# Start order, one transposed load and the last output segment of a one-core state-space and MLP kernel

## Chip, cores and metric

The kernel runs on 1 core of one Trainium2 chip. The metric is the device time of the program in microseconds; lower is better. Times below are medians of repeated runs, and readings of single instructions come from one profiled execution.

A core has five engines that run their own instruction streams and meet at semaphores: TensorE (PE in the profile; its weight loads are shown as PEld), VectorE (DVE), ScalarE (ACT), GpSimd (POOL) and SyncE (SP), which here only issues transfers. Transfers can also be issued from ScalarE's and GpSimd's streams.

## What is computed

```python
# scan: batch 4, 8 heads, 768 steps, head_dim D = 32, state N = 16
log_a = np.log(np.clip(a, 1e-06, 1.0))
for c in range(nc):                       # chunks of 32 steps
    cum = np.cumsum(la, axis=-1)
    L = np.exp(cum[:, :, :, None] - cum[:, :, None, :]) * causal
    M = np.einsum('bhin,bhjn->bhij', Cc, Bc) * L
    y_intra = np.einsum('bhij,bhjd->bhid', M, xc)
    y_inter = np.einsum('bhin,bhnd->bhid', Cc, state) * np.exp(cum)[..., None]
    y[:, :, sl] = y_intra + y_inter
    decay_from_j = np.exp(cum[:, :, -1:] - cum)
    Bx = np.einsum('bhjn,bhjd->bhjnd', Bc, xc) * decay_from_j[..., None, None]
    state = np.exp(la.sum(-1))[:, :, None, None] * state + Bx.sum(axis=2)
# bridge: (batch, heads, steps, D) -> 3072 tokens x 256
x = y.transpose(0, 2, 1, 3).reshape(3072, 256)
# MLP: w_in 256 x 2048, w_out 2048 x 256
h = x @ w_in
out = (h * (1 / (1 + np.exp(-h)))) @ w_out
```

`moe_w_in` and `moe_w_out` arrive as 64-bit floats; the kernel turns them into 32-bit floats itself.

## The kernel before

**Units and pairs.** The 3072 tokens are cut into 12 units of 256 (`UT`), three to a batch. A unit goes through the scan, then through the first product (`w_in` and silu, eight slots j of 256 hidden features each), then through the second (`w_out`). From the third pair of units on, the first product works on two units at once with seven products of half size in place of eight (`f_x1`); the second product of every pair does the same (`s2_pair`, segments named 1, w, 5, 7, 6, 4 and 3, each of eight matmul steps).

**The scan of a unit**, chunks of 64 steps (`Q`), by the names in the code:
- `f_Ab` (L308) spreads the decays over the partitions with two matmuls into a PSUM tile `hp`; `f_Ek` (L315, the scan of L303) turns them into the decay matrix E on VectorE. This pair of functions is used for units 0 and 1 only.
- B is needed twice. `bn` has tokens on the partitions (`load_n`, L99); `f_B` (L337) multiplies it by the last column of E on GpSimd. BH has states on the partitions: unit 0 loads `tbc` in blocks (`load_t`, L109) and transposes the 32x32 blocks on VectorE (`f_T`, L343, stream transposes at L346); unit 1 transposes `bn` itself on TensorE (`f_TP`, L350) and copies the result on ScalarE (L358). `f_T` and `f_TP` make CT from C in the same two ways, and `f_T2` (L361) makes the two masked copies `ce`.
- `f_D0` (L374) makes each chunk's state contribution, `f_G0` (L395) the products of C and B in the PSUM tile `gy`; `f_P01` (L274) makes the prefix products of units 0 and 1 on VectorE from the load `pa01`; `f_S` (L417) chains the states on VectorE (L428, L430); `f_SM` (L433) masks them; `f_M` (L412) multiplies E by `gy`; `f_Y` (L448) makes the output of the scan; `f_X` (L473) copies it to XM, in two halves for units 0 and 1.

**Weights** come in 16 pieces (0 to 7 of `w_in`, 8 to 15 of `w_out`). `load_w` fetches the raw words, `w_size` (L160) makes u and v on ScalarE, `w_bits` (L168) makes three VectorE instructions (L174, L176, L178) and the adds on GpSimd (L182; in two halves if `parts` is 2), and then issues the load of the piece seven further on. Slot j of the first product needs piece j.

**Order.** The program is laid out by hand (`manual_schedule`): what an engine does and in which order is the order of the calls. The start is L795 to L849: unit 0's scan, unit 1's scan woven with pieces 0 to 5, and the first four slots of unit 0 (`f_s1(0, 0)` to `f_s1(0, 3)`, L487). Then `steps` (L851) lists the other slots of units 0 and 1 as (unit, slot, what follows): "b5" is `w_bits(5)`, "s6" is `w_size(6)`. `busy(n, small)` (L222) issues matmuls on zeros, n of 512 columns and `small` of 64, which fill TensorE's gaps.

**PSUM.** `ps_h` has three buffers (tiles `hp`), `ps_s` one (`gy`), `ps_o` one (tiles `o_ps`: those of `busy`, of `f_TP` and of the second product). A tile of a pool waits until the readers of the tile that had its buffer before are done.

**The end.** L951 to L958 run `s2_pair(P, True)` for the last pair. Its segments give 128 output features on the partitions and 256 tokens in the free dimension. `end` (L572) copies each to `ps` (L578; the copy undoes the order in which `f_X` left the chunks), sums them on VectorE (`p_add`), and `f_out` (L550) transposes 32x32 blocks on VectorE and issues four transfers on SP. The last segment, "3", is the exception (L591 to L607): twice, for 128 tokens each, VectorE adds segment 6, TensorE transposes, ScalarE or VectorE copies, and SP or ScalarE issues a transfer.

Of the kernel before, what the change touches and what calls it, by code (L numbers as in the profile page):

```python
# [8 lines left out]
FP32 = mybir.dt.float32  # L9
# [3 lines left out]
ALU = mybir.AluOpType  # L13
# [8 lines left out]
def kernel(  # L22
# [56 lines left out]
    def at(u):  # L79
        return u // UPB, u % UPB * UT  # L80
# [28 lines left out]
    def load_t(u, i, q):  # L109

        b, t0 = at(u)
        if i == 0:
            tbc[u] = loads.tile([128, 2, 2, 8, N], FP32, name="tbc")
        for g in range(4):
            q.dma_start(out=tbc[u][32 * g:32 * g + 32, i],
                        in_=(B, C)[i][b, 2 * g:2 * g + 2, t0:t0 + UT].rearrange("e (t r) n -> t e r n", r=8))
# [42 lines left out]

    def w_size(n):  # L160
        if n in raw:
            u = wu[n] = wtp.tile([128, 2, WF], FP32, name="wu")
            v = wv[n] = wtp.tile([128, 2, WF], FP32, name="wv")
            nc.scalar.activation(u, raw[n][:, :, :, 1].bitcast(FP32), AF.Abs)

            nc.scalar.activation(v, raw[n][:, :, :, 0], AF.Copy, scale=2.0 ** -51, bias=2.0)

# [27 lines left out]
    pz01, one01, pfx01 = (flat[:, 8 * UT + QZ * i:8 * UT + QZ * (i + 1)] for i in range(3))  # L195
    load_t(0, 0, nc.scalar)
    load_t(0, 1, nc.sync)
# [117 lines left out]
    def f_Ek(u, k):  # L315
        scan_E(u, H * k, H, ab.pop((u, k)))
# [33 lines left out]
    def f_TP(u):  # L350

        tp = ps_o.tile([128, 512], FP32, name="o_ps")
        for i, t in enumerate((bn[u], tbc.pop(u))):
            for k in range(2):
                nc.tensor.transpose(out=tp[:, 256 * i + 128 * k:256 * i + 128 * k + 128],
                                    in_=t[:, k].rearrange("p h n -> p (h n)"), identity=ident)
        BH[u] = sc.tile([128, UT], FP32, name="bh")
        nc.scalar.activation(BH[u], tp[:, 0:256], AF.Copy)  # L358
        CT[u] = tp[:, 256:512]

# [112 lines left out]
    def f_X(u):  # L473
# [5 lines left out]
        for i in range(0, 4, n):  # L479
            nc.scalar.activation(XM[u][:, i:i + n], y[:, i:i + n, 0:128], AF.Copy)  # L480

    def new_g():

        return gpool.tile([128, NF, UT], FP32, name="gT").rearrange("p (k j) t -> p k j t", k=2)
# [76 lines left out]
    def s2_pair(P, final=False, joint=False):  # L561
# [10 lines left out]
        def end(m, o):  # L572

            p[m] = ppool.tile([128, UT], FP32, name="ps")
            on = o.rearrange("p (c k t) -> p c k t", c=2, k=2)
            pn = p[m].rearrange("p (k c t) -> p c k t", c=2, k=2)
            if not (final and m == "3"):
                nc.scalar.activation(pn, on, AF.Copy)  # L578
            if m == "w":
# [8 lines left out]
            elif m == "4":  # L588
                p_add(p["4"], p["4"], p["7"], adder)
                PEND.append(partial(f_out, P, 1, 0, p["4"]))  # L590
            elif m == "3" and final:  # L591

                for k in range(2):
                    nc.vector.tensor_tensor(out=pn[:, :, k], in0=on[:, :, k],
                                            in1=p["6"].rearrange("p (k c t) -> p c k t", c=2, k=2)[:, :, k],
                                            op=ALU.add)

                    tp = ps_h.tile([128, 512], FP32, name="hp")[:, 0:128]
                    nc.tensor.transpose(out=tp, in_=p["3"][:, 128 * k:128 * k + 128], identity=ident)
                    ot = opool.tile([128, UT], FP32, name="ot")[:, 0:128]  # L600
                    if k == 0:
                        nc.scalar.activation(ot, tp, AF.Copy)
                    else:
                        nc.vector.tensor_copy(out=ot, in_=tp)
                    b, t0 = at(2 * P + 1)
                    r = b * S + t0 + 128 * k
                    (nc.sync, nc.scalar)[k].dma_start(out=out[r:r + 128, 0:128], in_=ot)  # L607
            elif m == "3":
                p_add(p["3"], p["3"], p["6"], adder)
                PEND.append(partial(f_out, P, 0, 1, p["3"]))  # L610
# [12 lines left out]
        for n, (m, w, g) in enumerate(segs):  # L623
            if joint and n < 2:
                continue
            if final and n % 2 == 0:
# [148 lines left out]
    def scan_plan(G):  # L775
        plan = [([], [], []) for _ in range(8)]
        for i in range(2):
# [10 lines left out]
            plan[j + 2][2].append(partial(f_Y, u))  # L788
            plan[j + 3][1].append(partial(f_X, u))
            if u + 1 < NU:  # L790
# [3 lines left out]

    for i in range(2):  # L795
        f_T(0, i)
    for e in range(2):
        f_T2(0, e)
    f_Ab(0, 0)
    f_Ab(0, 1)  # L800
    busy(0, 20)
    f_G0(0)
    busy(4, 8)
    f_Ek(0, 0)
# [12 lines left out]
    w_size(1)  # L817
    busy(4, 17)
    f_Y(0)
    f_Ab(1, 1)  # L820
    f_X(0)
# [3 lines left out]
    f_s1(0, 0)  # L825
    f_Ek(1, 0)
    f_TP(1)
# [12 lines left out]
    for k in range(2):  # L840
        f_M(1, k)
    f_s1(0, 2)
    w_size(4)
    w_bits(3, 2)
    w_bits(4)
    f_Y(1)
    f_X(1)
    w_size(5)
    f_s1(0, 3)  # L849

    steps = ((1, 0, "b5 s6"), (1, 1, "b6 s7"), (1, 2, "b7 s8"), (1, 3, "b8"), (0, 4, ""),  # L851
             (1, 4, "T"), (0, 5, "E D s9"), (1, 5, "C b9 s10"), (0, 6, ""), (1, 6, "G b10 s11"),
# [137 lines left out]
```

## Time and profile before

| | us |
|---|---|
| median of 5 runs | 351.89 (351.63 to 352.75) |
| the profiled execution | 351.78 |
| its span | 350.1 |
| TensorE busy | 343.7 |
| VectorE busy | 205.5 |
| ScalarE busy | 162.4 |
| GpSimd busy | 112.4 |

The span is the time from the first to the last instruction that the profiler saw; the device time has a little around it. A line of the order of time gives start, duration, engine, line, operation, out <- in, shapes and count; several instructions of one kind that follow each other are one line whose duration runs from the first start to the last end. In brackets stands how long the engine was idle before and what ended that. The end of a matmul is modelled, so consecutive matmuls overlap in the records; their starts are what counts.

### The profile page before, as it was taken

The numbers are of one execution on the slowest core, as the hardware profiler recorded it, in microseconds if no ns is written. First come the engines' busy times: TensorE is split into PE (matmuls) and PEld (weight loads), VectorE is DVE, ScalarE is ACT, GpSimd is POOL, SyncE is SP. The second block draws the span as 40 slices with busy tenths as digits, with TensorE's granted clock in tenths as the row PEclk, the third lists the DMA queues.
The fourth block names the chain that finished last, engine by engine and source line by source line (L and its number), as shares of the span: only waits on it lengthen the run. The fifth ranks groups of instructions, "written<-read, shape, count | busy, mean of one in ns | idle before, by whom it ended". The sixth has DMA issues, their size and how long they took to land.

```text
span 350.1 us, 8359 instructions
## 1 busy us (share of the span) xinstructions
PE 343.7 (98%) x3308; PEld 287.5 (82%) x3308; DVE 205.5 (59%) x408; ACT 162.4 (46%) x396; POOL 112.4 (32%) x140
## 2 busy tenths in 40 slices
PE   8989999999999999999999999999999999999995
PEld 3568888888888888888888888888888888888884
DVE  6998899976795664544663563664552231234812
ACT  2578495323323545455645454644545454454100
POOL 4344346444185032244042244042234112051200
PEclk9999999999999999999999999999999999999999
DMA  5878897699866798956189955057404237522202
GB/s 107 213 221 217 228 324 125 120 208 224 145 123 116 127 169 148 189 111 98 21 160 162 179 102 103 16 106 138 93 2 75 52 55 147 94 39 41 43 1 46
DMA packets 117376, 42.79 MB, mean 122 GB/s; under 512 B 102488, under 2 KB 109144, under 8 KB 117336
## 3 DMA queue, kind: packets, MB, share of 16 engines
q1 hardware_dynamic: 110328, 25.67, 35.5%
q0 software_dynamic: 4464, 16.25, 25.0%
q10 hardware_dynamic: 2544, 0.33, 0.6%
q8 instruction: 26, 0.43, 0.5%
q14 instruction: 14, 0.11, 0.1%
HBM read 22.83 MB, written 3.15 MB: 74 GB/s over the span
## 4 chain that ended last, share of the span: by engine, by line
PE 92%; SPq 4%; DMA 2%; DVE 1%; issue 0%; ACT 0%; ACTq 0%; POOL 0%; DVEq 0%
PE o_ps L631 36%; PE hp L686 28%; PE hp L495 15%; PE hp L631 3%; PE gy L467 3%; PE o_ps L617 2%; PE gy L458 2%; PE gy L404 2%; SPq L107 2%; PE gy L389 1%; SPq L156 1%; DMA tbc<-in_C_dram 1%; DMA tbc<-in_B_dram 1%; DMA out_dram<-ot 0%; SPq L556 0%
## 5 line engine op out<-in xcount | busy, mean ns | idle before, releaser
L689 DVE TENSOR_TENSOR gT<-hp,p 128x256 f32<-128x256 f32 x64 | 26.9, 420 | 73.8 <-ACT p L700 37.8
L631 PE MATMUL o_ps<-gT,w_out_sb 128*128 128x256 f32 x240 | 60.4, 379 | 0.0
L692 ACT ACTIVATE gT<-gT 128x256 f32<-128x256 f32 x96 | 39.7, 414 | 43.9 <-DVE gT L689 43.8
L495 PE MATMUL hp<-XM,w_in_sb 128*128 128x256 f32 x256 | 59.3, 381 | 0.3 <-POOL w_in_sb L182 0.3
L495 PEld LDWEIGHTS hp<-XM,w_in_sb 128*128 128x128 f32 x256 | 47.8, 190 | 8.1 <-POOL w_in_sb L182 1.1
L686 PE MATMUL hp<-raw 128*128 128x256 f32 x192 | 52.7, 380 | 0.0
L548 POOL TENSOR_TENSOR ps<-ps 128x256 f32<-128x256 f32 x35 | 29.3, 838 | 71.2 <-ACT ps L578 69.9
L631 PEld LDWEIGHTS o_ps<-gT,w_out_sb 128*128 128x128 f32 x240 | 45.4, 190 | 6.3
L543 POOL DMA_DIRECT2D gT<-gT x31 | 27.3, 911 | 66.3 <-DVE TN L534 21.5
L686 PEld LDWEIGHTS hp<-raw 128*128 128x128 f32 x192 | 36.2, 190 | 5.4 <-POOL ps L548 0.6
L700 ACT ACTIVATE p<-hp 128x256 f32<-128x256 f32 x64 | 24.5, 383 | 27.4 <-PE hp L686 25.9
L689 DVE TENSOR_TENSOR gT<-hp,u 128x256 f32<-128x256 f32 x32 | 13.6, 425 | 38.9 <-PE hp L686 38.9
L686 PE MATMUL hp<-XM,w_in_sb 128*128 128x256 f32 x128 | 34.1, 389 | 0.0
L497 ACT ACTIVATE gT<-hp 128x512 f32<-128x512 f32 x32 | 18.9, 592 | 25.2 <-PE hp L495 25.2
L686 PEld LDWEIGHTS hp<-XM,w_in_sb 128*128 128x128 f32 x128 | 23.3, 190 | 4.3 <-issue 1.0
L303 DVE TENSOR_TENSOR_SCAN E<-ab,diag 128x256 f32<-128x256 f32 (+1 forms) x32 | 25.3, 832 | 0.4
L578 ACT ACTIVATE ps<-o_ps 128x256 f32<-128x256 f32 x38 | 14.4, 382 | 23.9 <-PE o_ps L631 19.8
L340 POOL TENSOR_TENSOR BT<-bn,E 128x256 f32<-128x256 f32 x12 | 9.4, 784 | 48.4 <-DVE E L303 39.3
L631 PE MATMUL o_ps<-gT,wu 128*128 128x256 f32 x88 | 22.4, 380 | 0.0
L631 PE MATMUL o_ps<-gT,wv 128*128 128x256 f32 x88 | 22.2, 380 | 0.0
L631 PE MATMUL o_ps<-gT,raw 128*128 128x256 f32 x80 | 20.5, 380 | 0.0
L686 PE MATMUL hp<-raw,w_in_sb 128*128 128x256 f32 x64 | 19.1, 380 | 0.0
(125 smaller groups left out, 521.1 us busy)
## 6 DMA issues: line engine op xcount, KB each, us to landing
gT<-gT POOLq DMA_DIRECT2D x31, 512.0 KB, 6.2
ab<-in_a_dram SPq DMA_DIRECT2D x40, 128.0 KB, 3.2
raw<-in_moe_w_in_dram SPq DMA_DIRECT2D x8, 512.0 KB, 5.8
raw<-in_moe_w_out_dram SPq DMA_DIRECT2D x8, 512.0 KB, 5.9
xt<-in_x_dram SPq DMA_DIRECT2D x24, 128.0 KB, 5.4
out_dram<-ot SPq DMA_DIRECT2D x92, 32.0 KB, 1.7
bn<-in_B_dram SPq DMA_DIRECT2D x22, 64.0 KB, 3.8
tbc<-in_C_dram SPq DMA_DIRECT2D x40, 32.0 KB, 5.5
```

The costliest lines, as they stand in the source:

```text
L303: nc.vector.tensor_tensor_scan(out=E[u].rearrange("p k h t -> p (k h t)")[:, Q * g0:Q * (g0 + n)], data0=t.rearrange("p g t -> p (g t)"), ...
L467: nc.tensor.matmul(out=y[32 * q:32 * q + 32, 2 * w + c, 64 * k:64 * k + 64], lhsT=xc[64 * c:64 * c + 64, k, h], rhs=m[64 * c:64 * c + 64, ...
L495: nc.tensor.matmul(out=hp[:, i], lhsT=w_in_sb[:, kc, f * 128:(f + 1) * 128], rhs=xm[:, kc], start=(kc == 0), stop=(kc == KC - 1))
L497: nc.scalar.activation(GTS[g][:, :, j], hp, AF.Silu)
L543: nc.gpsimd.dma_start(out=o[:, js], in_=a[:, js], accum_op=ALU.add)
L548: engine.tensor_tensor(out=o, in0=p, in1=q, op=op)
L578: nc.scalar.activation(pn, on, AF.Copy)
L631: nc.tensor.matmul(out=o, lhsT=w(j), rhs=g()[:, j], start=(j == 0), stop=(j == last))
L686: nc.tensor.matmul(out=o, lhsT=w, rhs=x_, start=start, stop=True, skip_group_check=True)
L689: nc.vector.tensor_tensor(out=o, in0=p, in1=q, op=ALU.add)
L692: nc.scalar.activation(o, i, AF.Silu)
L700: nc.scalar.activation(o, i, AF.Copy)
```

## The change

Four edits.

1. **B of unit 0.** The blocked load of B for unit 0 (four transfers on ScalarE's queue) and its VectorE transpose go. `f_TP(0)` makes BH on TensorE and ScalarE from `bn`, behind unit 0's two `f_Ab`; C of unit 0 stays as it was. The fillers of the start are cut anew.
2. **E of unit 1.** `f_Ek(1, 0)` moves from behind `f_s1(0, 0)` to just behind `f_Y(0)`, that is ahead of `w_bits(1, 2)` on VectorE.
3. **Slots.** `f_s1(1, 0)` runs ahead of `f_s1(0, 3)`. `w_size(4)` is split: u where it was, v behind `f_X(1)`, and `w_bits(4)` behind that.
4. **The last segment.** In segment "3" of the last pair the activations are the stationary operand and the weights the moving one, so that tokens come out on the partitions: per half of 128 tokens eight products of 128 columns. Segment 6, which has to be added, is transposed by TensorE in the midst of the first half and copied to `ps`. Each half is then one VectorE add and one transfer on SP. So that 128 consecutive tokens lie together, the last pair's XM is written in token order (`f_XN`, two copies in place of one), and the last pair's `end` copies without reordering.

```diff
     def load_t(u, i, q):
...
-        if i == 0:
+        if u not in tbc:
             tbc[u] = loads.tile([128, 2, 2, 8, N], FP32, name="tbc")
...
-    def w_size(n):
+    def w_size(n, what="uv"):
         if n in raw:
-            u = wu[n] = wtp.tile([128, 2, WF], FP32, name="wu")
-            v = wv[n] = wtp.tile([128, 2, WF], FP32, name="wv")
-            nc.scalar.activation(u, raw[n][:, :, :, 1].bitcast(FP32), AF.Abs)
-
-            nc.scalar.activation(v, raw[n][:, :, :, 0], AF.Copy, scale=2.0 ** -51, bias=2.0)
+            if "u" in what:
+                u = wu[n] = wtp.tile([128, 2, WF], FP32, name="wu")
+                nc.scalar.activation(u, raw[n][:, :, :, 1].bitcast(FP32), AF.Abs)
+            if "v" in what:
+                v = wv[n] = wtp.tile([128, 2, WF], FP32, name="wv")
+
+                nc.scalar.activation(v, raw[n][:, :, :, 0], AF.Copy, scale=2.0 ** -51, bias=2.0)
...
-    load_t(0, 0, nc.scalar)
     load_t(0, 1, nc.sync)
     load_n(0, 0, nc.scalar)
...
     def f_TP(u):
 
         tp = ps_o.tile([128, 512], FP32, name="o_ps")
-        for i, t in enumerate((bn[u], tbc.pop(u))):
+        for i, t in enumerate((bn[u],) if u == 0 else (bn[u], tbc.pop(u))):
...
         nc.scalar.activation(BH[u], tp[:, 0:256], AF.Copy)
-        CT[u] = tp[:, 256:512]
+        if u > 0:
+            CT[u] = tp[:, 256:512]
...
+    def f_XN(u):
+
+        XM[u] = xmp.tile([128, 4, 128], FP32, name="XM")
+        y = DP.pop(u)
+        for w in range(2):
+            nc.scalar.activation(XM[u][:, 2 * w:2 * w + 2].rearrange("p k (c t) -> p c k t", c=2),
+                                 y[:, 2 * w:2 * w + 2, 0:128].rearrange("p c (k t) -> p c k t", k=2), AF.Copy)
...
             p[m] = ppool.tile([128, UT], FP32, name="ps")
-            on = o.rearrange("p (c k t) -> p c k t", c=2, k=2)
-            pn = p[m].rearrange("p (k c t) -> p c k t", c=2, k=2)
-            if not (final and m == "3"):
-                nc.scalar.activation(pn, on, AF.Copy)
+            if final:
+                nc.scalar.activation(p[m], o, AF.Copy)
+            else:
+                nc.scalar.activation(p[m].rearrange("p (k c t) -> p c k t", c=2, k=2),
+                                     o.rearrange("p (c k t) -> p c k t", c=2, k=2), AF.Copy)
...
-            elif m == "3" and final:
-
-                for k in range(2):
-                    nc.vector.tensor_tensor(out=pn[:, :, k], in0=on[:, :, k],
-                                            in1=p["6"].rearrange("p (k c t) -> p c k t", c=2, k=2)[:, :, k],
-                                            op=ALU.add)
-
-                    tp = ps_h.tile([128, 512], FP32, name="hp")[:, 0:128]
-                    nc.tensor.transpose(out=tp, in_=p["3"][:, 128 * k:128 * k + 128], identity=ident)
-                    ot = opool.tile([128, UT], FP32, name="ot")[:, 0:128]
-                    if k == 0:
-                        nc.scalar.activation(ot, tp, AF.Copy)
-                    else:
-                        nc.vector.tensor_copy(out=ot, in_=tp)
-                    b, t0 = at(2 * P + 1)
-                    r = b * S + t0 + 128 * k
-                    (nc.sync, nc.scalar)[k].dma_start(out=out[r:r + 128, 0:128], in_=ot)
...
+            if final and m == "3":
+
+                for c in range(2):
+                    ts = slice(128 * c, 128 * c + 128)
+                    o = ps_h.tile([128, 512], FP32, name="hp")[:, ts]
+                    for j in range(NF // 2):
+                        nc.tensor.matmul(out=o, lhsT=g()[:, j, ts], rhs=w(j), start=(j == 0), stop=(j == last))
+                        if c == 0 and j == 3:
+
+                            q = ps_h.tile([128, 512], FP32, name="hp")
+                            for k in range(2):
+                                tk = slice(128 * k, 128 * k + 128)
+                                nc.tensor.transpose(out=q[:, tk], in_=p["6"][:, tk], identity=ident)
+                            p[m] = ppool.tile([128, UT], FP32, name="ps")
+                            nc.scalar.activation(p[m], q[:, 0:UT], AF.Copy)
+                        if j == last:
+                            nc.vector.tensor_tensor(out=p[m][:, ts], in0=o, in1=p[m][:, ts], op=ALU.add)
+                            b, t0 = at(2 * P + 1)
+                            r = b * S + t0 + 128 * c
+                            nc.sync.dma_start(out=out[r:r + 128, 0:128], in_=p[m][:, ts])
+                        if j % 2:
+                            yield
+                continue
...
-            plan[j + 3][1].append(partial(f_X, u))
+            plan[j + 3][1].append(partial(f_XN if G == NU // 2 - 1 else f_X, u))
...
-    for i in range(2):
-        f_T(0, i)
+    f_T(0, 1)
     for e in range(2):
         f_T2(0, e)
     f_Ab(0, 0)
     f_Ab(0, 1)
-    busy(0, 20)
+    f_TP(0)
+    busy(0, 18)
     f_G0(0)
-    busy(4, 8)
+    busy(2, 10)
     f_Ek(0, 0)
...
     w_size(1)
-    busy(4, 17)
+    busy(3, 18)
     f_Y(0)
+
+    f_Ek(1, 0)
     f_Ab(1, 1)
     f_X(0)
     w_size(2)
     w_bits(1, 2)
     load_unit(2)
     f_s1(0, 0)
-    f_Ek(1, 0)
     f_TP(1)
...
     f_s1(0, 2)
-    w_size(4)
+    w_size(4, "u")
     w_bits(3, 2)
-    w_bits(4)
     f_Y(1)
     f_X(1)
+    w_size(4, "v")
+    w_bits(4)
     w_size(5)
-    f_s1(0, 3)
-
-    steps = ((1, 0, "b5 s6"), (1, 1, "b6 s7"), (1, 2, "b7 s8"), (1, 3, "b8"), (0, 4, ""),
+
+    steps = ((1, 0, ""), (0, 3, "b5 s6"), (1, 1, "b6 s7"), (1, 2, "b7 s8"), (1, 3, "b8"), (0, 4, ""),
```

## The prediction

> **What bounds the kernel now.** I read the page's parts 1 and 4 first, then a table of stretches, then the order of time at both ends.
>
> ```profile
> PE 343.7 (98%) x3308; PEld 287.5 (82%) x3308; DVE 205.5 (59%) x408; ACT 162.4 (46%) x396; POOL 112.4 (32%) x140
> PE 92%; SPq 4%; DMA 2%; DVE 1%; issue 0%; ACT 0%; ACTq 0%; POOL 0%; DVEq 0%
> 10.00:15.00 5.00, 4.52 (x113) 2.60 (x113) 4.75 (x12) 3.60 (x8) 1.39 (x2) 1.00 0.98 288
> 15.00:20.00 5.00, 4.59 (x21) 3.28 (x20) 4.97 (x7) 3.00 (x7) 3.08 (x5) 1.00 0.78 121
> 20.00:25.00 5.00, 4.31 (x142) 3.20 (x142) 4.69 (x12) 3.78 (x8) 1.70 (x3) 1.00 0.73 252
> 30.00:321.00 291.00, 291.00 (x2767) 248.27 (x2766) 165.87 (x336) 142.61 (x355) 96.01 (x111) 1.00 0.65 124
> 343.00:350.10 7.10, 3.51 (x16) 2.51 (x14) 1.62 (x5) 0.28 (x1) 0.00 (x0) 1.00 0.26 52
> ```
>
> In the stretches the columns are PE, PEld, DVE, ACT and POOL busy, then granted clock and DMA. From 25.5 to 345.9 us TensorE never pauses, and the change takes no matmul out of that stretch. So time can only come from the two ends: from when the solid stretch begins (before 25 us, where VectorE is busy 14.41 of 15 us and sets the pace) and from what follows the last matmul.
>
> ```profile
> 4.82 0.64 DVE L346 STREAM_TRANSPOSE bh<-tbc 128x256 f32<-128x256 f32 x1
> 8.74 0.46 DVE L276 TENSOR_SCALAR gT<-gT 128x512 f32<-128x512 f32 x1 [0.55 <-DMA gT<-in_a_dram]
> 11.76 0.72 PE L227 MATMUL o_ps<-gT 128*64 128x64 bf16 x17
> 13.18 0.43 DVE L176 TENSOR_SCALAR wu<-wu 128x512 uint32<-128x512 uint32 x1
> 14.58 0.83 DVE L176 TENSOR_SCALAR wu<-wu 128x512 uint32<-128x512 uint32 x1
> 15.34 1.21 DVE L178 SCALAR_TENSOR_TENSOR wv<-raw,wv 128x512 uint32<-128x512 uint32 x1
> 16.47 2.32 DVE L303 TENSOR_TENSOR_SCAN E<-hp,diag 128x512 f32<-128x512 f32 x2
> 16.63 1.40 POOL L182 TENSOR_TENSOR w_in_sb<-wu,wv 128x256 uint32<-128x256 uint32 x2 [0.63 <-DVE wv L178]
> 24.71 0.81 PE L467 MATMUL gy<-E,xt 64*32 64x64 f32 x60 [0.40 <-issue]
> ```
>
> The L176 of piece 0 takes 0.43 us; that of piece 1, beside GpSimd's adds (14.29 to 16.00), 0.83. The scans run beside the same adds in 2.32 for two, against 2.27 alone. The last line is a pause in unit 1's f_Y that nothing in the profile explains: its records stand still from about 24.1 to 24.7.
>
> ```profile
> 342.31 3.62 PE L631 MATMUL hp<-gT,raw 128*128 128x256 f32 x16
> 345.96 0.49 DVE L594 TENSOR_TENSOR ps<-hp,ps 128x128 f32<-128x128 f32 x2 [2.08 <-PE hp L631]
> 346.98 0.36 SPq L607 DMA_DIRECT2D out_dram<-ot  x1
> 347.58 0.37 ACTq L607 DMA_DIRECT2D out_dram<-ot  x1
> ```
>
> After the last matmul come an add, a transpose, a copy and a transfer, twice; the second copy also waits for an output buffer, so the last transfer is issued 1.62 us after the add starts, and the span ends 2.5 us after that issue starts.
>
> **The last segment.** Removed behind the last matmul: the step from add to last issue, 345.96 to 347.58 = 1.62 us. Put in its place: one add of 128 columns (the two of L594 take 0.49 overlapped, one 0.29) and 0.03 to the issue on SP, 0.32. Saved: 1.30. Added on TensorE ahead of it: two transposes of p["6"] (the four of L355 fill 37.69 to 38.13, 0.11 each) 0.22; their copy (0.38 on ScalarE) is hidden by the 0.9 us of matmuls left in the first half. And sixteen long instructions become thirty-two of half the columns, each with a full weight load. Today one takes 3.45/16 = 0.216. If half costs half, 32 x 0.108 = 3.45, no loss. No row of before has such a pair, a 128-column f32 load for 128 moving columns. The nearest balanced one is the filler L227, 64 weights for 64 columns: (0.72 - 0.20)/16 = 0.033 each, where L225's 512 columns run at (1.04 - 0.38)/3/512 = 0.43 ns a column, 0.0275 for 64. So a balanced pair pays some 5 ns: 32 x 0.113 = 3.62, +0.17. The bad bound is the load's own recorded length, 0.190 (L631 PEld), unhidden: 32 x 0.19 = 6.08, +2.63. I take +0.17, since L227 has the same balance. The first half's transfer queues on SP behind f_out's four issues, which end at 345.94, before the second half's at about 346.7, so it delays nothing. Net 1.30 - 0.22 - 0.17 = **0.9 us gained** (1.08 to -1.55).
>
> The Trainium skill speaks against this part: "TensorE: Matmul & The Clock Gate", section "Back-to-back issue gap", says that in a stream of load and matmul pairs 128 columns take about 81 ns where the matmul alone would take 56. By that ratio the estimate for 32 pairs is 5.0 us, and the segment would lose about 0.5 instead; the L227 row, 0.033 against 0.0275, has a much smaller ratio.
>
> **B of unit 0 by TensorE.** Removed: four transfers on ScalarE's queue (1.84 us of issuing) and one VectorE transpose (0.61 until the next starts). The B load for bn moves to 0.81 there, and SP sheds waits on outstanding transfers (0.5 and 0.3 at L115, 0.4 at L199, in SP's table of waits), so the prefix's input lands about 1 us sooner and L276's 0.55 wait goes. E's first scan starts near 5.4 instead of 5.92, but the second needs the second f_Ab, whose matmuls end at 6.81 either way: 6.85 to 7.98 against 8.19. Then the prefix, with no wait, is done at 9.7 instead of 10.4. Now the other side. f_TP(0) runs at 6.75 to 6.97, its copy on ScalarE at about 7.17 to 7.55, and the fillers behind it on TensorE write the same single o_ps buffer, so they wait until 7.6. From there 18 small (0.58), f_G0 (0.62), 2 large (0.43), 10 small (0.32) and three changeovers of 0.1 put f_D0 at 9.85 against 9.45, and its first result near 10.2, where VectorE's L428 stood at 10.39. Gain **0.2**; bounds 0.67, if f_D0 isn't late (9.72 for 10.39), and -0.2, if L428 needs all of f_D0's 0.45 and a late copy adds 0.25.
>
> **E between the pieces.** No instruction is added; 1.2 us of scan move ahead of piece 1. Lost beside GpSimd today: 0.40 and 0.52 on piece 1 (L176, L178), 0.31 on piece 2's L176 (0.74): 1.23. In the new order the adds of piece 0 run in 1.40 (the 16.63 row) under a 1.2 us scan, so piece 1's L174 meets their last 0.4; piece 2's L174 and L176 meet the last of piece 1's adds and f_B, 0.35 and 0.3. Some 1.05 remain: gain **0.15** (0 to 0.9, if no overlap is left but piece 2's). Piece 1 reaches GpSimd 0.2 us later by itself; s1(0,1) waits for it, and the 0.2 and 0.15 cover that. With both, f_M(1) ends near 22.9 instead of 23.2.
>
> **Slot order.** Today s1(0,3) follows f_Y(1) without a gap at 25.49 and so hides XM(1)'s copy (0.38 for each half). Slot (1,0) needs that copy: 0.2 to the last matmul's end, 0.38 of copy, less the overlap with the changeover, about 0.45 of idle TensorE. Against this, piece 3's first half leaves GpSimd at 24.71 + 0.73 = 25.44 today, no sooner than s1(0,3) needs it, so 0.1 to 0.15 would be lost in the old order anyway. Net cost **0.3** (bounds 0.5, and -0.1 if the 24.1 pause is gone and piece 3 would be the late one). Splitting piece 4's sizes takes 0.66 of ScalarE from in front of XM(1), which today waits for TensorE, not for them: nothing. Piece 4 is first used by s1(0,4), 8.6 us after 25.49 (five slots of 1.73), and its adds end at 28.67: a delay of 0.5 is hidden by those 5 us. The load that its w_bits issues on SP (piece 11) stands behind load_unit(2), whose issues last to 37.74, so it leaves no later. f_XN makes 2 x 0.38 of one 0.60, under 27 us of ScalarE idle before its L700 copies: nothing.
>
> **Sum.** The start gains 0.2 + 0.15 - 0.3 = 0.05, the tail 0.9. The profiled execution took 351.78 (span 350.10 and 1.68 around it); 351.78 - 0.95 = 350.83, and its time stands 0.11 under the median of the runs, 351.89: **350.9**.
>
> **Rivals.**
> 1. *The start pays in full.* The pause in f_Y(1) (0.6) goes, because it hung on something that now falls elsewhere, or f_D0 isn't late (0.45 more). For it: VectorE's whole row from 10.4 to 23.2 is one chain, so each tenth at its head arrives. Against: the pause sits behind the same instructions. 350.9 - 0.45 to 0.6, about 350.3; both together 349.9.
> 2. *Slower: the weight loads are not hidden.* Place: the thirty-two pairs. At 0.190 a pair the tail loses 1.55, and the time is 350.9 + 0.9 + 1.55 = 353.3. It breaks even in the tail at (3.45 + 1.08)/32 = 0.142 a pair and makes the kernel slower by over 0.7 us from 0.165 on. For it: PEld shows 0.190, longer than the 0.108 beside which it must hide. Against: L227, where a load recorded with 0.113 (PEld) hides but for 0.005.
> 3. *The start loses what the tail gains.* f_D0 late and XM(1) uncovered, with no contention gained: 0.2 + 0.5 lost, 351.89 + 0.7 - 0.9 = 351.7. For it: both waits stand in program order. Against: VectorE loses a transpose and a 0.55 wait.
>
> **Chances.** Forecast 0.45 (its own range 350.5 to 351.3), rival 1: 0.22, rival 2: 0.14, rival 3: 0.19. A change under 0.2%, 0.7 us, can't be told from none, so faster is below 351.2: nearly all of the forecast (0.40) and all of rival 1, 0.62. Same: the forecast's rest, rival 3, and the mild part of rival 2: 0.26. Slower: 0.12. Range 349.9 to 352.3: rival 1's far end below; above, rival 3 and the part of rival 2 under 0.157 a pair.
>
> **What would show it.** Tail: thirty-two matmuls of 128 columns starting about 0.113 apart, and one issue 0.35 after the last of them ends. Start: L276 with no wait for the transfer; fillers of L227 starting near 7.6; L428 at 10.2; L178 of piece 1 at 0.69; the second f_M(1) ending near 22.9; a gap of 0.45 on TensorE before s1(1,0), which starts near 25.5. The forecast is wrong if the pairs stand 0.14 apart or more, if the gap before s1(1,0) exceeds 0.8, or if a pause appears after 30 us, where I assume none.

## The result and the profile after

| | before | after |
|---|---|---|
| median, us | 351.78 (57 runs, 351.34 to 353.37) | 350.49 (32 runs, 349.91 to 355.34) |
| the profiled execution | 351.78 | 351.28 |
| its span | 350.1 | 349.6 |
| TensorE / VectorE busy | 343.7 / 205.5 | 342.1 / 204.9 |

The ratio is 0.9967, 95% interval 0.9959 to 0.9976: 1.29 us less in the medians. The times of after form two groups, 349.9 to 350.7 and 351.0 to 351.5, with two runs far above; the execution that was profiled belongs to the upper group. Its gain of 0.50 us is therefore less than the median's, and the first question is what took the rest.

Line numbers have moved: L174, L176, L178 of `w_bits` are L176, L178, L180; the adds of GpSimd L182 are L184; L276 is L277; L303 (scan) L304; L428 (first copy to st) L430; L467 (f_Y) L469; L495 (first product) L505; the last segment's L631 is L626.

Parts 1 and 4 of the page of after, and the table of stretches (columns as before, with 40 to 50 us added):

```profile
PE 342.1 (98%) x3324; PEld 288.3 (82%) x3324; DVE 204.9 (59%) x406; ACT 162.8 (47%) x399; POOL 112.3 (32%) x140
PE 86%; SPq 4%; DVE 3%; DMA 3%; issue 2%; ACT 1%; POOL 0%; DVEq 0%; ACTq 0%
10.00:15.00 5.00, 4.46 (x115) 2.80 (x114) 4.63 (x11) 4.12 (x10) 1.95 (x3) 1.00 0.93 229
15.00:20.00 5.00, 4.48 (x52) 3.33 (x50) 4.92 (x9) 2.81 (x7) 2.61 (x5) 1.00 0.99 224
20.00:25.00 5.00, 4.39 (x153) 3.41 (x138) 4.51 (x10) 3.57 (x9) 2.00 (x4) 1.00 0.52 170
30.00:321.00 291.00, 290.08 (x2762) 247.38 (x2762) 165.78 (x336) 141.92 (x355) 95.58 (x111) 1.00 0.64 123
40.00:50.00 10.00, 9.08 (x93) 7.27 (x91) 8.45 (x17) 6.29 (x13) 2.19 (x2) 1.00 0.94 338
343.00:349.60 6.60, 3.51 (x32) 3.32 (x30) 1.45 (x4) 0.53 (x2) 0.00 (x0) 0.99 0.30 59
```

The stretch from 30 to 321 us, which was solid before, has lost 0.92 us of TensorE, all of it between 40 and 50 us. The chain that ended last, followed back from the end, leaves TensorE at that wait, near 45 us, where in before it stayed on TensorE down to some 21 us; this is why its share falls from 92% to 86%. The order of time shows how the start earned something and where it was lost again:

```profile
3.37 2.64 PE L312 MATMUL hp<-gT 108*128 108x512 f32 x4
5.37 2.27 DVE L304 TENSOR_TENSOR_SCAN E<-hp,diag 128x512 f32<-128x512 f32 x2
6.78 0.73 PE L228 MATMUL o_ps<-gT 128*64 128x64 bf16 x18 [0.55 <-ACT bh L359]
7.78 0.86 DVE L277 TENSOR_SCALAR gT<-gT 128x512 f32<-128x512 f32 x1
9.84 0.20 DVE L430 COPY st<-hp 128x64 f32<-128x64 f32 x1
13.81 1.22 DVE L304 TENSOR_TENSOR_SCAN E<-hp,diag 128x512 f32<-128x512 f32 x1 [0.15 <-PE gy L469]
15.82 0.68 DVE L180 SCALAR_TENSOR_TENSOR wv<-raw,wv 128x512 uint32<-128x512 uint32 x1
19.78 0.35 PE L391 MATMUL hp<-xt,BT 64*32 64x64 f32 x16 [0.15 <-DMA xt<-in_x_dram]
23.43 0.86 PE L469 MATMUL gy<-E,xt 64*32 64x64 f32 x64
24.76 1.56 PE L505 MATMUL hp<-XM,w_in_sb 128*128 128x256 f32 x6 [0.47 <-ACT XM L482]
40.90 0.69 DVE L322 TENSOR_SCALAR ab<-ab 128x1024 f32<-128x1024 f32 x1 [2.62 <-DMA ab<-in_a_dram]
44.41 0.92 POOL L341 TENSOR_TENSOR BT<-bn,E 128x256 f32<-128x256 f32 x1 [6.69 <-DMA raw<-in_moe_w_out_dram]
45.38 0.43 PE L391 MATMUL gy<-xt,BT 64*32 64x64 f32 x24 [0.92 <-POOL BT L341]
```

The first slot behind f_Y(1) starts at 24.76 instead of 25.49. At 45.38 TensorE, ahead of its old schedule, stands still for 0.92 us in f_D0(2): B of unit 2 comes from GpSimd, that needs the scan E, and the scan needs the transfer of `ab`, for which VectorE waits 2.62 us. (The line of f_B, L341, names another transfer; but f_B starts 0.22 us after the end of the scan in every one of the profiles, so the scan is what it waits for.) In the profile of before the same steps were

```profile
40.48 0.69 DVE L321 TENSOR_SCALAR ab<-ab 128x1024 f32<-128x1024 f32 x1 [1.02 <-DMA ab<-in_a_dram]
43.99 0.93 POOL L340 TENSOR_TENSOR BT<-bn,E 128x256 f32<-128x256 f32 x1 [5.09 <-DMA raw<-in_moe_w_out_dram]
45.13 0.43 PE L389 MATMUL gy<-xt,BT 64*32 64x64 f32 x24
```

and B was done at 44.92, 0.21 before f_D0(2) needed it. Of the 0.92, 0.46 come from TensorE's earlier arrival (44.46 for 45.13, less that slack) and 0.42 from the transfer's later one (40.90 for 40.48). f_B itself takes 0.92 or 0.93 in before, after and undo_Ek and 0.64 or 0.65 in all other profiles; what lengthens it isn't shown. So unit 2 begins 0.25 later than before, in spite of a start 0.73 sooner. The end of after:

```profile
342.56 1.05 PE L626 MATMUL hp<-raw,gT 128*128 128x128 f32 x8
343.67 2.84 PE L626 MATMUL hp<-raw,gT 128*128 128x128 f32 x24
346.01 1.22 SPq L639 DMA_DIRECT2D out_dram<-ps  x2
346.55 0.29 DVE L636 TENSOR_TENSOR ps<-hp,ps 128x128 f32<-128x128 f32 x1 [1.43 <-PE hp L626]
```

Taking the last matmul's duration as 0.27, the pairs stand (2.84 - 0.27)/23 = 0.112 us apart. From the first matmul of the segment to the issue of the last transfer it is 4.31 us (342.56 to 346.87), where it was 5.27. From that issue to the end of the span, however, it is 2.69, where it was 2.48. The profile's difference adds up: +0.25 at unit 2, -0.96 in the last segment, +0.21 at the exit, -0.50.

### The profile page after: what moved, and what is told of

Its sections match the earlier page's. It is cut to its first block, busy times and chain, and to the rows that moved or that the text cites. A ratio compares the mean times of both kernels' runs of the same rounds, so it can differ in the third digit from the quotient of the medians.

```text
span 349.6 us, 8382 instructions
## 1 busy us (share of the span) xinstructions
PE 342.1 (98%) x3324; PEld 288.3 (82%) x3324; DVE 204.9 (59%) x406; ACT 162.8 (47%) x399; POOL 112.3 (32%) x140
## 4 chain that ended last, share of the span: by engine, by line
PE 86%; SPq 4%; DVE 3%; DMA 3%; issue 2%; ACT 1%; POOL 0%; DVEq 0%; ACTq 0%
PE o_ps L648 36%; PE hp L703 28%; PE hp L505 9%; PE hp L648 3%; PE gy L469 2%; PE o_ps L611 2%; PE gy L406 2%; SPq L107 2%; PE gy L460 2%; SPq L156 1%; DMA xt<-in_x_dram 1%; DMA raw<-in_moe_w_out_dram 1%; PE gy L391 1%; PE hp L626 1%; DVE wv L180 1%
## 5 line engine op out<-in xcount | busy, mean ns | idle before, releaser
L505 PE MATMUL hp<-XM,w_in_sb 128*128 128x256 f32 x256 | 59.3, 381 | 0.8 <-ACT XM L482 0.5
L505 PEld LDWEIGHTS hp<-XM,w_in_sb 128*128 128x128 f32 x256 | 48.0, 190 | 8.6 <-POOL w_in_sb L184 1.3
L507 ACT ACTIVATE gT<-hp 128x512 f32<-128x512 f32 x32 | 18.9, 594 | 26.7 <-PE hp L505 26.6
L304 DVE TENSOR_TENSOR_SCAN E<-ab,diag 128x256 f32<-128x256 f32 (+1 forms) x32 | 25.1, 827 | 0.8 <-DVE ab L323 0.5
L341 POOL TENSOR_TENSOR BT<-bn,E 128x256 f32<-128x256 f32 x12 | 9.5, 795 | 47.3 <-DVE E L304 37.3
L588 ACT ACTIVATE ps<-o_ps 128x256 f32<-128x256 f32 x35 | 13.3, 382 | 14.8 <-PE o_ps L648 11.8
```

What stands on the lines that cost most here:

```text
L304: nc.vector.tensor_tensor_scan(out=E[u].rearrange("p k h t -> p (k h t)")[:, Q * g0:Q * (g0 + n)], data0=t.rearrange("p g t -> p (g t)"), ...
L341: engine.tensor_tensor(out=BT[u], in0=bn[u], in1=E[u][:, :, :, Q - 1:Q].to_broadcast([128, 2, H, N]), op=ALU.mult)
L505: nc.tensor.matmul(out=hp[:, i], lhsT=w_in_sb[:, kc, f * 128:(f + 1) * 128], rhs=xm[:, kc], start=(kc == 0), stop=(kc == KC - 1))
L507: nc.scalar.activation(GTS[g][:, :, j], hp, AF.Silu)
L588: nc.scalar.activation(p[m].rearrange("p (k c t) -> p c k t", c=2, k=2), o.rearrange("p (c k t) -> p c k t", c=2, k=2), AF.Copy)
```

## The experiments

All kernels were timed beside before on the same chip (three chips; medians of before there 351.78, 351.90 and 351.87). undo_Ek, rot4 and rot4_undo_Ek have five runs, tail_only eight, the others eleven or twelve.

| kernel | chip | median (range), us | ratio to before, 95% interval |
|---|---|---|---|
| tail_only | first | 350.87 (350.55 to 352.16) | 0.9977, 0.9966 to 0.9989 |
| start_only | first | 352.17 (351.45 to 353.50) | 1.0014, 1.0003 to 1.0026 |
| ab_first | first | 350.99 (350.56 to 352.01) | 0.9982, 0.9971 to 0.9992 |
| old_slots | first | 351.35 (350.78 to 352.70) | 0.9988, 0.9978 to 0.9997 |
| after_again | second | 350.81 (349.88 to 354.22) | 0.9977, 0.9958 to 0.9996 |
| no_warm | second | 352.66 (350.55 to 352.95) | 1.0012, 0.9998 to 1.0025 |
| undo_B | second | 351.01 (350.24 to 352.19) | 0.9978, 0.9967 to 0.9988 |
| undo_Ek | second | 350.24 (350.13 to 351.11) | 0.9964, 0.9953 to 0.9976 |
| after_third | third | 350.88 (350.22 to 352.42) | 0.9964, 0.9941 to 0.9987 |
| tail_again | third | 351.13 (350.86 to 351.65) | 0.9979, 0.9968 to 0.9990 |
| rot4 | third | 350.50 (350.35 to 350.90) | 0.9966, 0.9954 to 0.9978 |
| rot4_undo_Ek | third | 350.51 (350.02 to 350.99) | 0.9965, 0.9952 to 0.9978 |

Each left one profiled execution. Six points of each, us: the moment from which the trace's records of the granted clock show TensorE at full speed (the first such record; before it there is none, and the column of the granted clock prints 1.00 there too), the start of the fourth matmul of the start (the last of unit 0's two f_Ab), of the first copy to st, of the first slot behind f_Y(1), of f_D0(2), and the time from the issue of the last transfer to the end of the span.

| kernel | full clock from | f_Ab | st | first slot | f_D0(2) | exit | time |
|---|---|---|---|---|---|---|---|
| before | 6.43 | 6.00 | 10.39 | 25.49 | 45.13 | 2.48 | 351.78 |
| tail_only | 4.89 | 5.44 | 10.41 | 25.52 | 45.16 | 2.46 | 350.82 |
| tail_again | 5.03 | 5.61 | 10.62 | 25.72 | 45.36 | 2.46 | 351.01 |
| start_only | 5.17 | 5.64 | 9.69 | 24.36 | 43.99 | 2.94 | 351.45 |
| after | 4.76 | 5.42 | 9.84 | 24.76 | 45.38 | 2.69 | 351.28 |
| after_again | 6.92 | 5.99 | 10.51 | 25.39 | 45.02 | 2.70 | 350.90 |
| after_third | 7.06 | 5.96 | 10.56 | 25.25 | 44.88 | 2.70 | 351.19 |
| ab_first | 6.84 | 6.02 | 10.48 | 25.15 | 44.78 | 2.84 | 351.50 |
| old_slots | 4.98 | 5.50 | 9.80 | 25.32 | 44.95 | 2.71 | 351.02 |
| undo_B | 5.91 | 5.94 | 10.07 | 25.15 | 45.09 | 2.49 | 350.77 |
| undo_Ek | 5.40 | 5.72 | 9.77 | 24.75 | 45.13 | 2.71 | 351.06 |
| rot4 | 5.33 | 5.72 | 9.77 | 24.82 | 44.45 | 2.46 | 350.39 |
| rot4_undo_Ek | 4.51 | 5.30 | 9.56 | 24.96 | 44.59 | 2.46 | 350.34 |
| no_warm | 12.19 | 5.95 | 12.41 | 27.09 | 46.72 | 2.70 | 352.62 |

**The tail alone** has the start of before with the fourth edit. Two places of its difference from after:

```diff
-    f_T(0, 1)
+    for i in range(2):
+        f_T(0, i)
...
-    steps = ((1, 0, ""), (0, 3, "b5 s6"), (1, 1, "b6 s7"), (1, 2, "b7 s8"), (1, 3, "b8"), (0, 4, ""),
+    steps = ((1, 0, "b5 s6"), (1, 1, "b6 s7"), (1, 2, "b7 s8"), (1, 3, "b8"), (0, 4, ""),
```

> The kernel before with the fourth edit alone (last segment with tokens on the partitions, f_XN, plain copies in end). In the profiled runs the stretch from the first matmul of the last segment to the end of the span fell from 7.79 to 7.04 us. Theory (the two ends add up, each by itself): 351.78 - 0.75 = 351.0, ratio 0.998, and the times lie as close together as those of before. Rival (the tail gains only if the start has shifted something in front of it, such as the transfers of f_out): under 0.4 gained.

The median is 0.91 under before, and in the second run of the same kernel, below, 0.74. Unit 2 begins at 45.16, as before, and the profiled execution is 0.96 faster. The tail accounts for most of the gain.

**The start alone** has the first three edits and the last segment of before.

> The changed kernel with the last segment of before. Theory: the start brings slot (1,0) forward by 0.74 us (24.76 against 25.50), but f_D0 of unit 2 then waits for that unit's ab load, by 0 to 0.9 us from run to run; so times between 351.0 (no wait) and 351.9 (the wait of the profiled run), the median near 351.2. Rival (the wait is a matter of the one profiled run): nearly all times near 351.0.

Neither came. Its profiled execution, the fastest of its twelve, is the best start of all (slot at 24.36, f_D0(2) at 43.99, 1.14 sooner than before), yet it is only 0.33 faster than before's profiled execution: 0.2 goes in a wait at 101 us, some 0.15 between the last matmul and the last issue, and 0.46 in the exit (2.94 for 2.48). The median is 0.39 above before. What happened in its slower executions no profile shows. On its own the start brings nothing in the time (1.0014, 1.0003 to 1.0026), and why it is even a little slower stays open.

**The load of unit 2 ahead.** `ab` of unit 2 is issued before its C and B; f_TP(2) moves behind slot (1,5).

```diff
     def load_unit(u):
         load_pa(u, nc.sync)
+        if u == 2:
+            load_ab(u, nc.sync)
...
-        load_ab(u, nc.sync)
+        if u != 2:
+            load_ab(u, nc.sync)
...
-             (1, 4, "T"), (0, 5, "E D s9"), (1, 5, "C b9 s10"), (0, 6, ""), (1, 6, "G b10 s11"),
+             (1, 4, ""), (0, 5, "E D s9"), (1, 5, "T C b9 s10"), (0, 6, ""), (1, 6, "G b10 s11"),
```

> The changed kernel; load_unit(2) issues ab of unit 2 ahead of C and B in place of behind them, and f_TP(2) with f_T2 moves one slot later, behind slot (1,5). Theory (the ab load of unit 2 bounds f_D0(2), and its landing varies): f_E0(2) no longer waits for a transfer, the gap of 0.9 us ahead of f_D0(2) is gone, the times near 351.3 are gone and the median is 350.2 or less. Rival (the two groups of times, near 350.3 and near 351.3, come from when TensorE's clock rises at the start: the four matmuls of f_Ab take 2.64 us in one profile and 3.45 in the other): both groups stay, the median stays near 350.5.

The wait for B is gone and another is in its place, on the transposed C that now comes later:

```profile
45.68 0.70 PE L409 MATMUL gy<-ce,bh 32*64 32x128 f32 x32 [0.47 <-ACT ce L370]
```

The times spread from 350.56 to 352.01, and both forecasts of the median, 350.2 and 350.5, were too low. So this is no cure, and the wait for `ab` can't be the whole of the upper group. Over the table, f_D0(2) waits in after (0.92), undo_Ek (0.68) and undo_B (0.25), and not in after_again, after_third, rot4 or rot4_undo_Ek: the transfer's arrival moves from run to run (VectorE's use of it starts from 39.82 in rot4 to 40.90 in after), and TensorE meets it or not.

Unit 2 is not the only place where a sooner start is spent. From f_D0(2) to the f_D0 that stands at 252.36 in before, it is 207.23 us in before, tail_only, tail_again, after, after_again and undo_B, and longer by 0.28 in rot4 (TensorE waits 0.21 for B at 101 us), 0.42 in after_third (it waits at 48 us, on ScalarE's L507) and 0.68 in ab_first, 0.47 of it the wait above.

**The old order of slots**: the third edit undone whole, all else as in after.

```diff
-    w_size(4, "u")
+    w_size(4)
     w_bits(3, 2)
+    w_bits(4)
     f_Y(1)
     f_X(1)
-    w_size(4, "v")
-    w_bits(4)
     w_size(5)
...
+    f_s1(0, 3)
-    steps = ((1, 0, ""), (0, 3, "b5 s6"), (1, 1, "b6 s7"), (1, 2, "b7 s8"), (1, 3, "b8"), (0, 4, ""),
+    steps = ((1, 0, "b5 s6"), (1, 1, "b6 s7"), (1, 2, "b7 s8"), (1, 3, "b8"), (0, 4, ""),
```

> The changed kernel with the slot order of before: f_s1(0,3) behind f_X(1), w_size(4) whole and w_bits(4) ahead of f_Y(1). By the profile of the changed kernel f_Y(1) ends its issue at 24.1 to 24.3 us, piece 3's first half leaves GpSimd at 24.87 and XM(1)'s first half is there at 24.71. Theory: slot (0,3) starts at 24.9 in place of slot (1,0) at 24.76, and the two w_size(4) instructions ahead of XM(1) delay nothing: 0.1 slower to equal, 350.5 to 350.6. Rival, from the prediction (the slot order costs 0.3 because XM(1) is uncovered): 0.3 faster, 350.2.

The old order is not faster; at 351.35 it lies above both forecasts. Its first slot hides XM(1) and waits for weights instead, 0.63 where the new order waits 0.47:

```profile
25.32 0.91 PE L505 MATMUL hp<-XM,w_in_sb 128*128 128x256 f32 x3 [0.63 <-POOL w_in_sb L184]
```

From the end of the second f_M(1) (23.06) to the first slot it is 2.26, as in before (23.23 to 25.49); in after it is 2.10 (22.66 to 24.76). The new order gains 0.16. tail_again, which has the start of before unaltered, shows the same wait for piece 3:

```profile
25.72 1.57 PE L506 MATMUL hp<-XM,w_in_sb 128*128 128x256 f32 x6 [0.62 <-POOL w_in_sb L184]
```

In before, tail_only and tail_again TensorE pauses in f_Y(1) for 0.40, 0.17 and not at all, and the first slot comes 2.26, 2.26 and 2.25 after f_M(1). So in the old order the pause cost nothing. The ratio, 0.9988, lies above that of after (0.9967) by more than this; the profile of old_slots also has a wait for x of unit 1 ahead of f_M(1), which the order of these slots, later, doesn't set.

**After, unaltered**, as the measure for the next three kernels.

> The changed kernel again, unaltered, so that the three beside it are compared on one chip. Two groups of times as before: near 350.3 and near 351.3, median 350.5 to 350.9.

Here is the second face of the start. The order of time of this execution:

```profile
3.37 3.69 PE L312 MATMUL hp<-gT 108*128 108x512 f32 x4
7.09 1.22 DVE L304 TENSOR_TENSOR_SCAN E<-hp,diag 128x512 f32<-128x512 f32 x1 [0.48 <-PE hp L312]
7.74 0.73 PE L228 MATMUL o_ps<-gT 128*64 128x64 bf16 x18 [0.47 <-ACT bh L359]
10.51 0.23 DVE L430 COPY st<-hp 128x64 f32<-128x64 f32 x1 [0.28 <-PE hp L391]
```

The four f_Ab matmuls take 3.69 from first start to last end instead of 2.64, VectorE waits 0.48 for the second, the fillers start at 7.74, f_D0 comes late, and the first copy to st starts 0.67 later than in the first profile, 0.12 later than in before. Nothing in the program differs. The matmuls start 0.92, 0.85 and 0.85 apart, where those of the first profile stand 0.98, 0.65 and 0.43 apart: TensorE's clock rose among them there and after them here. The records of the granted clock agree: full speed from 4.76 in the first profile and from 6.92 in this one.

The two groups of times did not come back clearly. Eleven runs of after_again lie between 349.88 and 351.36 and one at 354.22, and those of after_third, below, between 350.22 and 352.42; in both some stand between the two groups (350.72, 350.90 and 350.93; 350.79 and 350.98). Nor does the clock sort the profiled times: after_again, with the late clock, took 350.90, and after, with the early one, 351.28.

**No warming.** The five 512-column fillers ahead of the start are left out; they compute nothing that is used.

```diff
-    busy(5)
```

> The changed kernel without the five filler matmuls of busy(5) ahead of f_Ab, which compute nothing that is used. In the six profiles so far the four matmuls of f_Ab of unit 0 start at a spacing of 0.85 to 0.98 us until TensorE's clock rises and at 0.43 afterwards; the last of them starts at 5.42 to 5.64 us in four profiles and at 6.00 or 6.02 in two. Theory (the changed start has no VectorE transpose left that covers f_Ab, so the second scan of E waits for f_Ab's last matmul, and the group of times near 351.3 is the one with the late clock): without the fillers the clock never rises in time, the last f_Ab matmul starts at 5.9 or later in every run, and nearly all times are near 351.3 or above. Rival (the upper group is the wait of f_D0(2) for its ab load): the median stays within 0.3 of that of the unaltered kernel.

```profile
7.05 1.23 DVE L303 TENSOR_TENSOR_SCAN E<-hp,diag 128x512 f32<-128x512 f32 x1 [0.48 <-PE hp L311]
7.91 1.12 PE L228 MATMUL o_ps<-gT 128*64 128x64 bf16 x18 [0.47 <-ACT bh L358]
12.41 0.22 DVE L429 COPY st<-hp 128x64 f32<-128x64 f32 x1 [2.23 <-PE hp L390]
```

The eighteen small fillers take 1.12 instead of 0.73, and the first copy to st waits 2.23 us for f_D0. The time is 1.85 us above after_again. The four f_Ab are no later than in after_again (5.95 and 5.99); what is later is the rise of the clock, at 12.19 us, so that the fillers and f_D0 run at the low clock too. The experiment thus shows that the start pays for a late clock, but it overshoots: it says nothing on whether the runs near 351.3 are those with a rise near 7. With B of unit 0 on TensorE, the start hangs on how soon the clock rises. In before it did not: with the rise at 6.43 st starts at 10.39, and in tail_only and tail_again, with the rise at 4.89 and 5.03 and an early fourth f_Ab (5.44, 5.61), at 10.41 and 10.62, since the two transposes and their loads hold up VectorE ahead of the scan (in tail_again the transpose of C waits 0.40 for its load).

**B of unit 0 back to VectorE.**

```diff
+    load_t(0, 0, nc.scalar)
     load_t(0, 1, nc.sync)
...
-        for i, t in enumerate((bn[u],) if u == 0 else (bn[u], tbc.pop(u))):
+        for i, t in enumerate((bn[u], tbc.pop(u))):
...
+    f_T(0, 0)
     f_T(0, 1)
...
-    f_TP(0)
-    busy(0, 18)
+    busy(0, 20)
...
-    busy(2, 10)
+    busy(4, 8)
...
-    busy(3, 18)
+    busy(4, 17)
```

> The changed kernel with the first edit undone (B of unit 0 loaded in blocks and transposed on VectorE, old fillers); E between the pieces, the slot order and the last segment stay. Theory (VectorE's transpose covers f_Ab again, so the clock at the start doesn't matter, but the head of the VectorE chain is 0.2 to 0.55 us later): median 350.8 to 351.0, that is between the unaltered changed kernel and the last segment alone (350.87), and a narrower spread than that of the changed kernel. Rival (the first edit brings nothing): the same median as the changed kernel.

0.20 above after_again in the median, with intervals that overlap; the narrower spread did not come (350.24 to 352.19). The exit is 2.49 again. st starts at 10.07, between after's early execution (9.84) and its late ones (10.51, 10.56). The clock rose at 5.91 here, between theirs too, so how the two paths compare at one and the same clock isn't shown.

**E of unit 1 back to its old place.**

```diff
-    f_Ek(1, 0)
     f_Ab(1, 1)
...
     f_s1(0, 0)
+    f_Ek(1, 0)
     f_TP(1)
```

> The changed kernel with the second edit undone (f_Ek(1,0) behind f_s1(0,0) again). Theory of the prediction (moving the scan saves 0.15 us of contention, bounds 0 to 0.9): 0.1 to 0.2 slower than the changed kernel beside it; L178 and L180 of piece 1 take about 0.83 and 1.2 again. Rival (the profile of the changed kernel shows 12.82 us from f_S's first instruction to the end of f_M(1), against 12.84 before, because f_Ek(1,0) now waits for f_Y(0) and f_S(1) for f_D0(1)): no difference over 0.1.

Piece 1 again meets GpSimd's adds, and the first slot, at 24.75, is where after has it:

```profile
13.98 0.83 DVE L178 TENSOR_SCALAR wu<-wu 128x512 uint32<-128x512 uint32 x1
14.74 1.22 DVE L180 SCALAR_TENSOR_TENSOR wv<-raw,wv 128x512 uint32<-128x512 uint32 x1
```

From st to the end of the second f_M(1) this kernel takes 12.87, after 12.82, before 12.84. In executions of the new place in which TensorE doesn't wait for x of unit 1 (after_third, ab_first, start_only) that stretch is 12.56 to 12.58. So the scan's place is worth at most 0.3, and nothing or less when x is late: in old_slots, where TensorE waits 0.53 for x, the stretch is 13.25. The time doesn't show a gain: the median is 0.57 below that of after_again, where the theory had it 0.1 to 0.2 above, from five runs whose interval overlaps.

**The exit.** In the records of the trace SP ends the program with a row of nine semaphore instructions, some 0.06 us apart unless one has to wait, and about 0.9 us of closing instructions behind them. The four loads of `load_t(0, 0)` that after lacks may change which semaphore the last transfer gets. rot4 puts four transfers back, of 4 bytes each, which nothing reads:

```diff
+    turn = const.tile([1, 4], FP32, name="turn")
+    for n in range(4):
+        nc.sync.dma_start(out=turn[:, n:n + 1], in_=bass.AP(tensor=a.tensor, offset=a.offset, ap=[[1, 1], [1, 1]]))
     for G in range(2, NU // 2):
```

> after with four more transfers of 4 bytes each on SP's queue, issued between the slots of unit 3 and the loop over the later pairs of units, into a tile that nothing reads; all else as in after. Theory (exit: the semaphores of the transfers are used in turn by eight, and with four loads fewer the last transfers' semaphore is looked at early in SP's closing row of waits, with four looks of about 0.06 us behind it): from the issue of the last transfer to the end of the span 2.45 to 2.50 us instead of 2.69, and the median 0.2 us under that of the unaltered after of the same call. Rival (the exit's length is set by the transfers themselves, and the order of the looks is an accident): 2.70 stays, and the medians agree within 0.15 us.

> after unaltered, to be compared with the others on the same chip. Median 350.3 to 350.8, exit 2.70 us.

The nine semaphore instructions of that row, start in us:

```
after_third  347.18 347.25 347.38 347.76 348.35 348.41 348.47 348.53 348.59   span ends 349.48
rot4         346.62 346.69 346.75 346.82 346.88 346.94 347.00 347.20 347.80   span ends 348.68
```

In after_third the fifth waits last, and four more follow it, 0.06 each; in rot4 the ninth waits last. From the issue of the last transfer to that instruction it is the same (346.78 to 348.35, 346.22 to 347.80). The exit is 2.46 against 2.70: that 0.24 us is the row's order is shown. The other profiles agree: the six kernels with the four loads or the four small transfers have 2.46 to 2.49, the eight without either 2.69 to 2.94. In the times the medians are 0.38 apart, but the ratios, 0.9966 and 0.9964, are not: the timing doesn't resolve it.

> The start of before with the fourth edit alone, once more, beside after on the same chip. Theory (the three edits of the start bring in the time only a little, 0.1 to 0.4 us, part of which the exit takes back): median 0.1 to 0.4 us above after's, exit 2.46. Rival (the start's slot (1,0), 0.74 us sooner in the profile, counts in full): 0.7 us above after's. Second rival (the start brings nothing): within 0.1 us of after's.

Median 0.25 above after_third: the theory's size, though the intervals overlap (0.9968 to 0.9990 and 0.9941 to 0.9987).

> after with the second edit undone (the scan E of piece 1 of unit 1 back behind the slot of unit 0) and the four small transfers. If both what the exit costs and the scan's new place are worth what single runs said (0.2 and 0 to 0.5 us), the median is 0.2 to 0.6 us under after's on the same chip and this is the fastest version; if the scan's place is worth nothing and the exit is an accident, it agrees with after within 0.15 us.

It agrees with rot4 (350.51 and 350.50) and by its ratio with after: no version was found that is surely better than after. In the profile of rot4_undo_Ek the pause in f_Y(1) is back (0.39 us between two starts, up to 23.68), and in the new order of slots it costs: the first slot comes 2.53 after f_M(1), where after has 2.10.

## Why the prediction was right, and where its steps were not

The predicted 350.9 lies 0.4 above the median of after and within 0.1 of its two later runs (350.81, 350.88), and the tail carries it as forecast. The start was put at 0.05. What it is worth in the time isn't resolved: the tail alone has ratios of 0.9977 and 0.9979, after 0.9967, 0.9977 and 0.9964, so 0 to 0.5 us with intervals that overlap, and alone it was 0.39 slower. That so small a sum fits is luck in part. In the profile of after the three edits bring the first slot 0.73 sooner, not 0.05, and unit 2 and the exit, which the sum didn't have, take 0.98 and 0.21.

- **The last segment: right.** 0.113 a pair was predicted, 0.112 measured; the two transposes cost 343.67 - 343.45 = 0.22, as predicted; last add to last issue 0.32. Predicted 0.9, measured 0.96 up to the last issue. Rival 2 (0.19 a pair) fell. The rule of the Trainium skill, "TensorE: Matmul & The Clock Gate", section "Back-to-back issue gap", whose ratio of 81 to 56 would have made each pair about 0.156 (an estimate), does not hold for these 128-column pairs of 32-bit floats.
- **"The span ends 2.5 us after that issue starts", taken as fixed: wrong** by 0.21 to 0.24. Four transfers more or fewer, far from the end of the program, set it.
- **B by TensorE, +0.2: right in mechanism, mis-sized.** The profile of before is one with a late clock (6.43), and the prediction took that clock for granted. The wait of the fillers for the copy was foreseen, and so was f_D0's lateness. What failed is "the second f_Ab, whose matmuls end at 6.81 either way": they end at 6.01 (3.37 + 2.64) or 7.06 (3.37 + 3.69) as the clock rises. Against before's 10.39, st gains 0.55 to 0.83 in the early executions and loses 0.09 to 0.17 in the late ones: about the two bounds stated, 0.67 and -0.2, and both occur.
- **E between pieces, +0.15: mis-sized, 0 to 0.3.** Piece 1 falls from 0.42, 0.84 and 1.22 (tail_only) to 0.49, 0.43 and 0.68, 0.88 saved, and its last instruction is the 0.69 predicted. Piece 2 rises from 1.83 in sum to 2.14, the overlap that the prediction listed (L176 of that piece takes 0.72 instead of 0.40). Two things it had not: the scan waits 0.15 for f_Y(0), because E has one buffer, and two separate scans take 2.44 where the pair took 2.32. 0.88 - 0.31 - 0.15 - 0.12 = 0.30, which is seen only where x of unit 1 doesn't come late.
- **Slot order, -0.3: wrong sign.** The gap before s1(1,0) is 0.47, as predicted (0.45). But the old order pays more, 0.63, for piece 3, where "0.1 to 0.15" was allowed; the pause at 24.1 us hid this in before, and in old_slots and tail_again, where the pause is gone, the wait for piece 3 takes its place, 0.63 and 0.62. Rival 1's 0.6 for that pause was thus nothing to be gained in the old order. The named bound, a gain of 0.1, was the right branch: 0.16.
- **"A pause appears after 30 us, where I assume none": it appeared.** B of unit 2 had 0.21 us of slack in before. A sooner start runs into it in some executions and waits up to 0.92 there.

So a gain of rival 1's size at the start, 0.73, was there in the profile of after (0.55 at st, 0.02 up to the end of f_M(1), 0.16 at the slot) and was given back at unit 2 and at the exit. How often each of the clock and the pause occurs, and so what makes the two groups of times, isn't settled: one profile for each kernel shows that both occur, not in what share.

## What to carry to other kernels

A gain at the start of a solid stretch counts only up to the next transfer that was just in time: measure the slack of the next unit's load before paying for a sooner start. At the end of a program count the chain behind the last matmul, instruction by instruction, for here it arrived in the time, 0.96 in the profile and 0.74 to 0.91 in the medians; swapping the operands so that the result needs no transpose behind the last matmul is what brought it. Before moving work from VectorE to TensorE in the first microseconds, ask whether the path then hangs on a clock that rises at no fixed time.

## What the runs showed of the hardware

- TensorE's clock rises at no fixed time after the program's start. Full clock is on record from between 4.51 and 7.06 us in thirteen profiles with the same five fillers ahead, and the fourth f_Ab starts between 5.30 and 6.02. From there to the drop at the end the full clock lasts 344.75 us in eleven of them and 341.33 in two, and 337.92 in no_warm: steps of 3.41 to 3.42. The Trainium skill, "TensorE: Matmul & The Clock Gate", section "What's actually happening", explains this by an activity window that runs freely and isn't reset when a kernel starts, and gives a spread of half a microsecond either way. A free-running window fits the steps; the spread of 2.55 us seen here is larger than the page's.
- The program's exit is a row of semaphore instructions that SP works off one after another, 0.06 us each, and its length depends on which of them belongs to the transfer that lands last. From the issue of the last transfer to the end it is 2.46 with the ninth waiting last (rot4) and 2.70 with the fifth (after_third); in ab_first it is 2.84, because there the fifth is also released later, 1.72 after the issue and not 1.57.
- GpSimd's f_B goes with a slower VectorE instruction, whichever it falls beside. In after it starts at 7.72: L277 takes 0.86 and the prefix's scan behind it 1.24; in after_third it starts at 8.37, L277, mostly ahead of it, takes 0.40 and the scan 1.56.
